# One head of wo on 64 partitions by eight small loads, w2's rows 8 to 13 in one slot, and LN2's sums on the vector engine, in a decode block on one core

## The chip, the core and the metric

The kernel runs on one NeuronCore of a Trainium2 chip. A core has TensorE (PE: matmuls; its weight loads are listed apart, as PEld), VectorE (DVE), ScalarE (ACT), GpSimd (POOL) and SyncE (SP, which here only issues DMAs), and sixteen DMA engines that move data from HBM to the on-chip memory (SBUF, 128 partitions). Matmuls write to PSUM. The metric is the device time of one execution in microseconds (us), the median of several runs.

## The reference, cut to what matters

Two sequences, one token each: a block with adaptive layer norm, attention over the last 4096 positions of a K/V cache, and a feed-forward with SiLU. All is fp32.

```python
def reference(A_x, A_k_cache, A_v_cache, A_wq, A_wo, B_x, B_w1, B_w2, c, w_mod):
    # B=2, D=512, 32 query heads, 8 KV heads, Dh=128, F=1792, window W=4096
    x = A_x
    mod = (silu(c) @ w_mod).reshape(2, 6, 1, -1)
    sa, ca, ga, sb, cb, gb = (mod[:, i] for i in range(6))
    h = layernorm(x) * (1 + ca) + sa
    x = x + ga * attention(h, A_k_cache, A_v_cache, A_wq, A_wo)   # last W keys; ends in  o @ wo
    h = layernorm(x) * (1 + cb) + sb                              # LN2
    return x + gb * (silu(h @ B_w1) @ B_w2)
```

The weights and the part of the caches that is read are 97.5 MB, each byte used once.

## The kernel before

Nearly all of the work is the loading. Every large load goes through one queue, SP's, into a ring of eight slots of 16 KB per partition (`slots`; `stream(n)` gives the next n). A load can be issued only when what stood in its slots has been read, so SP waits for PE before most loads. The order of the loads is w_mod, x, wq, then four groups (`grp` 0 to 3; a group is four KV heads of one sequence), for each group K and then V, 8 MB each in four slots, then wo in two loads (heads 0 to 23 and 24 to 31), w1 in two, and w2 in five: rows 0 to 7 of the fourteen that each partition holds, rows 8 to 10, 11, 12 and 13. `inorder` keeps an instruction in the order of the code on its engine.

For each group PE forms the scores (L281), softmax runs on DVE and ACT, PE forms the weighted sum of V (L326), and `collect` scales the result on ACT and turns it by PE into columns (`oT`, L345), which a copy puts into `oTn`: for each head a block of 128 partitions x 32 columns. After the last group:

- `acc_o` (L413): for each head q one matmul with `oTn[:, q]` stationary and the head's 512 columns of wo moving. The output goes to 32 of the 128 rows of `acc_o`, quarter g = q % 4, so that the four quarters of the array (32 columns each) can run side by side. The profile calls this shape 128*32.
- `gather` adds the four quarters up: ACT copies acc_o in two halves to `acc_o_sb` (L396), PE forms `ao` (L400). DVE turns it and forms `x1T`, the residual, as 128 x 4 x 2.
- LN2: `column_means` (L443) multiplies `x1T` with a matrix of 1/512 in four accumulating matmuls; `dT`, `hT` and `sq` follow on DVE. The product with w1 (`hid`, L459) runs on the unscaled h; the variance's `column_means` stands between its two halves, and the scale `rstd` comes in after the product.
- SiLU on DVE and ACT gives `uT` (L163).
- w2: the first WIDE = 11 rows go through `acc_yw` (L489), in quarters as with wo; ACT copies the sum to `y_sb` (L511). The last three rows are "turned" (L501): the weights are stationary and the two columns of uT move, sixteen small instructions for a row (eight for the first). The same is done with y_sb, between these rows. A scan on DVE (L522) and a store end it.
- `busy(n, ...)` puts n matmuls without use (L266, `junk`) on PE where it would wait. They write to rows 0 to 31, the first quarter.

Each fp32 matmul is two passes on PE and counts twice in the profile.

Of the kernel before, what the change touches and what calls it, by code (L numbers as in the profile page):

```python
# [8 lines left out]
F32 = mybir.dt.float32  # L9
# [4 lines left out]
P = 128  # L14
# [14 lines left out]
def adaln_block(  # L29
# [54 lines left out]

    def load_runs(w, per, lo, hi):

        e = w.shape[1]
        n = -(-(hi - lo) * e // 4096)
        t = stream(n)[:, : (hi - lo) * e].rearrange("p (q e) -> p q e", e=e)
        inorder(nc.sync.dma_start(t, w.rearrange("(p q) e -> p q e", q=per)[:, lo:hi, :]))  # L90
        return t
# [168 lines left out]

    oT = bank("O", "oT")[:, :64]
    STEPS = 4
# [72 lines left out]
    def collect(grp, o_ps, rl):  # L335

        o_sb = once.tile([P, 4 * DH], F32, tag="wide", name=f"ob{grp}")
        for c in (slice(0, D // 2), slice(D // 2, D)):
            nc.scalar.activation(o_sb[:, c], o_ps[:, c], AF.Copy, scale=rl)  # L339
        last = grp == STEPS - 1  # L340
        if last:
            busy(1, junk[0])
        cols = oT[:, 16 * grp : 16 * grp + 16]
        for v in range(4):
            inorder(nc.tensor.matmul(  # L345
                cols[:, 4 * v : 4 * v + 4],
                o_sb[:, v * DH : (v + 1) * DH],
                id4[:, 4 * v : 4 * v + 4],
                start=True,
                stop=True,  # L350
            ))
        b, n = divmod(grp, 2)
        (nc.vector.tensor_copy if last else nc.scalar.copy)(
            oTn[:, 16 * n : 16 * n + 16, 16 * b], cols
        )
# [3 lines left out]
    def load_wo(lo, hi):  # L359
        wt = load_runs(wo, 32, lo, hi)  # L360
        wot.extend(wt[:, q, :] for q in range(hi - lo))

    for grp in range(STEPS):
        s_ps = scores(grp)
        if grp < STEPS - 1:
            kt[grp + 1] = load_group(k_cache, grp + 1)
        else:
            load_wo(0, 24)
            load_wo(24, 32)
# [40 lines left out]
    busy(4, junk[0])  # L410
    for q in range(32):
        g = q % 4
        inorder(nc.tensor.matmul(  # L413
            acc[32 * g : 32 * g + 32, :],
            oTn[:, q, :],
            wot[q],
            start=(q < 4),
            stop=(q >= 28),
        ))
    gather(ao, acc, "acc_o_sb", True, True, fill=1)  # L420
    busy(1, junk[1])
    T2, WIDE = F // P, 11
    w2t = {}
    for lo, hi in ((0, 8), (8, 11), (11, 12), (12, 13), (13, T2)):
        wt = load_runs(w2, T2, lo, hi)
        for tt in range(lo, hi):
            w2t[tt] = wt[:, tt - lo, :]
    aoT = once.tile([P, 4, 32], F32, tag="zp", name="aoT")
# [10 lines left out]
    def column_means(t, name):  # L439

        m = bank("B", name)[:, :B]
        for k in range(4):
            inorder(nc.tensor.matmul(m, mean512, t[:, k, :], start=(k == 0), stop=(k == 3)))  # L443
        return m

    mean = column_means(x1T, "mean_b")
    busy(1, junk[1])
# [5 lines left out]
    sq = once.tile([P, 4, B], F32, tag="sq", name="sq")  # L453
    nc.vector.tensor_mul(sq, dT, dT)
    FC = F // 4
    hp = bank("A", "hid")[:, :FC]
    for k in range(4):
        for g in range(4):
            inorder(nc.tensor.matmul(  # L459
                hp[32 * g : 32 * g + 32, :],  # L460
                hT[:, k, :],
                w1t[k][:, g * FC : (g + 1) * FC],
                start=(k == 0),
                stop=(k == 3),
            ))
        if k == 1:
            var = column_means(sq, "var_b")
# [122 lines left out]
```

## Time and profile before

| what | value |
|---|---|
| time, median of 3 runs | 233.28 us (233.25 to 233.31) |
| the profiled execution | 233.04 us, its span 231.4 us |
| mean granted TensorE clock | 0.801 over the span, 1.00 from 202 us on |
| PE busy | 126.8 us (55%) |
| ACT, DVE, POOL busy | 19.7, 15.0, 7.7 us |
| DMA | 97.65 MB, mean 422 GB/s |

Span is the time from the first to the last instruction on the core. A row of a timeline has its start and its duration in us, the engine, the line of the code, the operation, out<-in and how many instructions were merged; behind it in brackets stands the idle time of the engine ahead of it and what ended that. "issue" means that the profile shows nothing that the engine waited for. Matmul durations overlap: a pass of 0.59 us leaves its part of the array earlier than that.

### The profile page before, as it was taken

How to read it: one execution, taken by the hardware profiler on the slowest of the kernel's cores; microseconds unless marked ns; L12 is line 12 of the kernel's file. 1: busy time of each engine (PE TensorE's matmuls, PEld its weight loads, DVE VectorE, ACT ScalarE, POOL GpSimd, SP SyncE). 2: the span in 40 equal slices, each digit the busy share in tenths (PEclk: the TensorE clock that was granted, in tenths of full speed). 3: DMA queues.
4: the chain of work that ended last, by engine and by line, in shares of the span. 5: the costliest groups of instructions: out<-in, count | busy, mean ns of one | idle time of the engine just before them, and what ended most of it. 6: DMA issues, size and time to landing. Idle time of an engine off the chain costs nothing.

```text
span 231.4 us, 2188 instructions
## 1 busy us (share of the span) xinstructions
PE 126.8 (55%) x982; PEld 45.9 (20%) x982; DVE 15.0 (6%) x44; ACT 19.7 (9%) x45; POOL 7.7 (3%) x28
## 2 busy tenths in 40 slices
PE   0005906831950781491096078139509607999986
PEld 0003301310210221121033012112202202345333
DVE  0004020000011000002000000100000200000130
ACT  0203010110040010001001000100100100000331
POOL 8102000000000000000000000000000000000000
PEclk9999995985796596598579659656957965999999
DMA  9998988989889898898999989999899999999993
GB/s 399 417 454 362 544 362 385 513 374 532 362 374 532 374 513 374 385 513 385 487 396 396 510 385 467 408 408 498 385 430 445 419 456 408 416 405 442 413 411 137
DMA packets 2915, 97.65 MB, mean 422 GB/s; under 512 B 460, under 2 KB 476, under 8 KB 1116
## 3 DMA queue, kind: packets, MB, share of 16 engines
q1 hardware_dynamic: 2748, 97.52, 97.9%
q8 instruction: 7, 0.11, 0.2%
q10 hardware_dynamic: 160, 0.01, 0.0%
HBM read 97.53 MB, written 0.01 MB: 421 GB/s over the span
## 4 chain that ended last, share of the span: by engine, by line
DMA 73%; PE 23%; POOL 2%; issue 1%; SPq 0%; ACT 0%; DVE 0%; POOLq 0%
DMA slots<-in_A_v_cache_dram 50%; PE o L326 16%; DMA slots<-in_A_wq_dram 13%; DMA slots<-in_B_w_dram 10%; PE q L235 4%; PE acc_yw L489 1%; PE yx L501 1%; PE qT L245 0%; POOL qs L136 0%; POOL oTn L140 0%; SPq L152 0%; ACT q_sb L243 0%; POOL warm L114 0%; POOL avg L104 0%; POOL same L108 0%
## 5 line engine op out<-in xcount | busy, mean ns | idle before, releaser
L326 PE MATMUL o<-slots,probs 128*32 128x512 f32 x256 | 37.9, 755 | 29.1 <-DMA slots<-in_A_v_cache_dram 29.1
L281 PE MATMUL s<-slots,qs 128*32 128x512 f32 x256 | 35.5, 718 | 32.3 <-DMA slots<-in_A_k_cache_dram 32.3
L326 PEld LDWEIGHTS o<-slots,probs 128*32 128x32 f32 x256 | 11.5, 131 | 52.2 <-issue 52.2
L281 PEld LDWEIGHTS s<-slots,qs 128*32 128x32 f32 x256 | 9.4, 130 | 55.2 <-issue 39.0
L235 PE MATMUL q<-slots,hq_T 128*32 128x512 f32 x64 | 9.2, 724 | 7.3 <-DMA slots<-in_A_wq_dram 7.3
L293 DVE TENSOR_REDUCE mx<-s 128x1 f32<-128x512 f32 x4 | 2.8, 691 | 140.5 <-PE s L281 140.5
L173 PE MATMUL mean_a<-mv_a,avg 128*128 128x1 f32 x2 | 0.6, 347 | 18.4 <-DVE mv_a L170 18.4
L266 PE MATMUL junk<-warm,id 128*32 128x512 f32 x20 | 9.6, 595 | 0.0
L339 ACT ACTIVATE ob<-o,rl 128x256 f32<-128x256 f32 x8 | 3.4, 470 | 69.4 <-PE o L326 69.4
L413 PE MATMUL acc_o<-slots,oTn 128*32 128x512 f32 x64 | 7.2, 593 | 0.0
L295 ACT ACTIVATE mp<-part,mx 128x8 f32<-128x8 f32 x4 | 1.2, 300 | 70.0 <-DVE mx L293 70.0
L209 PE MATMUL m_sp<-slots,scT 128*32 128x512 f32 x32 | 5.9, 827 | 0.0
L345 PE MATMUL oT<-id,ob 128*128 128x4 f32 x32 | 4.2, 255 | 1.9 <-ACT ob L339 1.9
L235 PEld LDWEIGHTS q<-slots,hq_T 128*32 128x32 f32 x64 | 2.3, 130 | 13.3 <-issue 13.2
L345 PEld LDWEIGHTS oT<-id,ob 128*128 128x128 f32 x32 | 3.9, 191 | 5.5 <-ACT ob L339 5.5
L308 PE MATMUL lp<-rowsum,same 128*128 128x1 f32 x8 | 1.7, 286 | 5.1 <-ACT pr L303 5.1
L206 PE MATMUL m_a<-slots,scT 128*32 128x256 f32 x32 | 3.6, 543 | 1.1 <-POOL scT L163 1.1
L413 PEld LDWEIGHTS acc_o<-slots,oTn 128*32 128x32 f32 x64 | 3.6, 110 | 3.3 <-issue 3.1
L173 PEld LDWEIGHTS mean_a<-mv_a,avg 128*128 128x128 f32 x2 | 0.5, 310 | 18.4 <-issue 18.4
L297 PE MATMUL mg<-mp,same 128*128 128x8 f32 x8 | 1.6, 266 | 4.6 <-ACT mp L295 4.6
L459 PE MATMUL hid<-slots,hT_b 128*32 128x448 f32 x32 | 3.4, 544 | 0.0
L489 PE MATMUL acc_yw<-slots,uT 128*32 128x512 f32 x22 | 2.8, 599 | 0.9 <-DMA slots<-in_B_w_dram 0.9
(95 smaller groups left out, 59.9 us busy)
## 6 DMA issues: line engine op xcount, KB each, us to landing
slots<-in_w_mod_dram SPq DMA_DIRECT2D x1, 6144.0 KB, 17.1
slots<-in_A_wo_dram SPq DMA_DIRECT2D x1, 6144.0 KB, 25.6
slots<-in_B_w_dram SPq DMA_DIRECT2D x1, 2688.0 KB, 17.8
slots<-in_A_wo_dram SPq DMA_DIRECT2D x1, 2048.0 KB, 29.6
slots<-in_B_w_dram SPq DMA_DIRECT2D x1, 2048.0 KB, 23.1
slots<-in_B_w_dram SPq DMA_DIRECT2D x1, 896.0 KB, 19.6
slots<-in_B_w_dram SPq DMA_DIRECT2D x1, 768.0 KB
slots<-in_B_w_dram SPq DMA_DIRECT2D x3, 256.0 KB, 16.0
```

The costliest lines, as they stand in the source:

```text
L206: nc.tensor.matmul(m_a[r, :], scT[:, k, :], ab[:, g], start=(k == 0), stop=(k == 3))
L209: nc.tensor.matmul(m_sp[r, :], scT[:, k, :], cd[:, g], start=(k == 0), stop=(k == 3))
L235: inorder(nc.tensor.matmul(q_ps[32 * g : 32 * g + 32, :], hq_T[:, k, :], wqt[:, k, lo : lo + 4 * DH], start=(k == 0), stop=(k == 3),))
L266: inorder(nc.tensor.matmul(unread[0:32, :], id4, warm, start=True, stop=True,))
L281: inorder(nc.tensor.matmul(s_ps[32 * c : 32 * c + 32, :], stat(grp, v, s), kt[grp][:, lo : lo + 512], start=(s == 0 and v == 0), stop=(s = ...
L293: nc.vector.tensor_reduce(mx, s_ps, axis=AX.X, op=ALU.max)
L326: inorder(nc.tensor.matmul(o_ps[r : r + 32, :], probs[grp % 2][:, 32 * n + 16 * s : 32 * n + 16 * s + 32], vt[grp][:, lo : lo + 512], star ...
L339: nc.scalar.activation(o_sb[:, c], o_ps[:, c], AF.Copy, scale=rl)
L345: inorder(nc.tensor.matmul(cols[:, 4 * v : 4 * v + 4], o_sb[:, v * DH : (v + 1) * DH], id4[:, 4 * v : 4 * v + 4], start=True, stop=True,))
L413: inorder(nc.tensor.matmul(acc[32 * g : 32 * g + 32, :], oTn[:, q, :], wot[q], start=(q < 4), stop=(q >= 28),))
L459: inorder(nc.tensor.matmul(hp[32 * g : 32 * g + 32, :], hT[:, k, :], w1t[k][:, g * FC : (g + 1) * FC], start=(k == 0), stop=(k == 3),))
L489: inorder(nc.tensor.matmul(yw[32 * g : 32 * g + 32, :], uT[:, tt, :], w2t[tt], start=(tt < 4), stop=(tt >= WIDE - 4),))
```

## The change

**One head of wo.** Head 27 (`SPLIT`) leaves the large wo tensor, which keeps 31 heads; its loads are now heads 0 to 23 of these 31 and the other seven. Head 27's 128 x 512 weights become a tensor `wo2` of eight pieces of 8 rows x 1024 elements (32 KB each), and after each of the eight K and V loads SP issues one of them, into eight partitions (p, p+4, ... p+28) of a new buffer `woh` of 64 partitions x 2 x 512. On SP, from the last group's loads to the last of w2, before:

```order
L82 DMA slots<-in_A_k_cache_dram 128x16384
L82 DMA slots<-in_A_v_cache_dram 128x16384
L90 DMA slots<-in_A_wo_dram 128x12288
L90 DMA slots<-in_A_wo_dram 128x4096
L90 DMA slots<-in_B_w_dram 128x5376
L90 DMA slots<-in_B_w_dram 128x1792
L90 DMA slots<-in_B_w_dram 128x4096
L90 DMA slots<-in_B_w_dram 128x1536
L90 DMA slots<-in_B_w_dram 128x512 x3
```

and now (5376 and 1792 are w1, what follows is w2):

```order
L84 DMA slots<-in_A_k_cache_dram 128x16384
L87 DMA woh<-in_A_wo_dram 8x1024
L84 DMA slots<-in_A_v_cache_dram 128x16384
L87 DMA woh<-in_A_wo_dram 8x1024
L98 DMA slots<-in_A_wo_dram 128x12288
L98 DMA slots<-in_A_wo_dram 128x3584
L98 DMA slots<-in_B_w_dram 128x5376
L98 DMA slots<-in_B_w_dram 128x1792
L98 DMA slots<-in_B_w_dram 128x4096
L98 DMA slots<-in_B_w_dram 128x1024
L98 DMA slots<-in_B_w_dram 128x512 x4
```

A small load now follows each K and each V load (those of the three earlier groups too), wo's second load is shorter by a head, and w2's rows 8 and 9 come as one load, the others alone. The large loads keep their order.

The head's output is needed on partitions 0 to 63 twice: its first 64 rows come there as they are, its last 64 rows by a fifth `oT` matmul in the groups 1 and 3, whose stationary window is shifted by 64 columns, as a 33rd block of `oTn`. In `acc_o` two matmuls over 64 partitions take the place of head 27's, at places 24 and 25, so that acc_o has 33 rows and its last one is in quarter 32 % 4 = 0.

On PE, from the turning of the last group's result to the gathering, before:

```order
L345 MATMUL oT<-id,ob_592 128x4 x4
L266 MATMUL junk_591<-warm,id 32x512 x4
L413 MATMUL acc_o<-slots,oTn 32x512 x32
L266 MATMUL junk_607<-warm,id 32x512
L400 MATMUL ao<-acc_o_sb,id 32x128 x4
L266 MATMUL junk_607<-warm,id 32x512
L443 MATMUL mean_b<-x1T,mean_87 128x2 x4
L266 MATMUL junk_607<-warm,id 32x512
L459 MATMUL hid<-slots,hT_b 32x448 x8
L443 MATMUL var_b<-sq,mean_87 128x2 x4
L459 MATMUL hid<-slots,hT_b 32x448 x8
L266 MATMUL junk_607<-warm,id 32x512 x2
```

and now:

```order
L365 MATMUL oT<-id,ob_602 128x1
L275 MATMUL junk_601<-warm,id 32x512 x4
L435 MATMUL acc_o<-slots,oTn 32x512 x24
L435 MATMUL acc_o<-woh,oTn 32x512 x2
L435 MATMUL acc_o<-slots,oTn 32x512 x7
L275 MATMUL junk_618<-warm,id 32x512
L419 MATMUL ao<-acc_o_sb,id 32x128 x4
L275 MATMUL junk_618<-warm,id 32x512
L470 MATMUL mean_b<-ks_mean_b,mean_87 128x2
L275 MATMUL junk_618<-warm,id 32x512
L487 MATMUL hid<-slots,hT_b 32x448 x8
L470 MATMUL var_b<-ks_var_b,mean_87 128x2
```

The two half rows stand inside acc_o, one oT matmul is added ahead of it, and mean_b and var_b have one matmul instead of four (the rows that end the piece are hid's second half and three junk matmuls instead of two).

**LN2's sums.** `column_means` first adds the four parts on DVE (`tensor_reduce`, 128x2 from 128x8) and then needs one matmul; for the variance the sum stands ahead of hid's first half in the code, the matmul where it was.

**w2.** Rows 8 to 13 go into one slot instead of four, in loads of rows 8 and 9, 10, 11, 12 and 13. WIDE is 10, so that row 10 is turned too. On PE at the end, before:

```order
L489 MATMUL acc_yw<-slots,uT 32x512 x11
L501 MATMUL yx<-uT,slots 64x2 x8
L501 MATMUL yx<-id,y_sb 32x2 x8
L501 MATMUL yx<-uT,slots 32x2 x16
L501 MATMUL yx<-id,y_sb 32x2 x8
L501 MATMUL yx<-uT,slots 32x2 x16
```

and now:

```order
L517 MATMUL acc_yw<-slots,uT 32x512 x10
L529 MATMUL yx<-uT,slots 64x2 x8
L529 MATMUL yx<-id,y_sb 32x2 x8
L529 MATMUL yx<-uT,slots 32x2 x16
L529 MATMUL yx<-id,y_sb 32x2 x8
L529 MATMUL yx<-uT,slots 32x2 x32
```

One row leaves acc_yw, and sixteen small matmuls are added behind the last part of y_sb.

The diff, without the host's rearranging of wo:

```diff
+SPLIT = 27
 def load_group(cache, grp):
     t = stream(4)
-    nc.sync.dma_start(t, cache[grp])
+    inorder(nc.sync.dma_start(t, cache[grp]))
+    i = 2 * grp + (cache is v_cache)
+    p = 32 * (i // 4) + i % 4
+    inorder(nc.sync.dma_start(
+        woh[p : p + 29 : 4, :, :].rearrange("p s e -> p (s e)"), wo2[i]
+    ))
     return t
...
-    oTn = const([P, 32, 32], "oTn")
+    woh = const([P // 2, 2, D], "woh")
+    oTn = const([P, 33, 32], "oTn")
...
     # collect
-    cols = oT[:, 16 * grp : 16 * grp + 16]
+    b, n = divmod(grp, 2)
+    per = 16 + n
+    cols = oT[:, 17 * grp : 17 * grp + per]
...
+    if n:
+        v = SPLIT % 16 // 4
+        inorder(nc.tensor.matmul(
+            cols[:, 16:17],
+            o_sb[:, v * DH + DH // 2 : v * DH + DH // 2 + DH],
+            id4[:, SPLIT % 16 : SPLIT % 16 + 1],
+            start=True, stop=True,
+        ))
...
-    for q in range(32):
-        g = q % 4
+    heads = [q for q in range(HQ) if q != SPLIT]
+    parts = [(oTn[:, q, :], wot[i]) for i, q in enumerate(heads)]
+    parts[24:24] = [(oTn[: P // 2, q, :], woh[:, i, :]) for i, q in enumerate((SPLIT, HQ))]
+    for i, (o, w) in enumerate(parts):
+        g = i % 4
         inorder(nc.tensor.matmul(acc[32 * g : 32 * g + 32, :], ...))
...
-    T2, WIDE = F // P, 11
-    for lo, hi in ((0, 8), (8, 11), (11, 12), (12, 13), (13, T2)):
-        wt = load_runs(w2, T2, lo, hi)
+    T2, WIDE = F // P, 10
+    wt = load_runs(w2, T2, 0, 8)
+    ends = stream()[:, : (T2 - 8) * D].rearrange("p (q e) -> p q e", e=D)
+    for lo, hi in ((8, 10), (10, 11), (11, 12), (12, 13), (13, T2)):
+        load_runs(w2, T2, lo, hi, ends[:, lo - 8 : hi - 8, :])
...
     def column_means(t, name):
+        ks = once.tile([P, B], F32, tag=f"ks_{name}", name=f"ks_{name}")
+        nc.vector.tensor_reduce(ks, t.rearrange("p k b -> p b k"), axis=AX.X, op=ALU.add)
         m = bank("B", name)[:, :B]
-        for k in range(4):
-            inorder(nc.tensor.matmul(m, mean512, t[:, k, :], start=(k == 0), stop=(k == 3)))
-        return m
+        return m, lambda: inorder(nc.tensor.matmul(m, mean512, ks, start=True, stop=True))
...
-    busy(2, junk[1])
+    busy(3, junk[1])
     hidT = ...
```

More of the change, by code (lines that the diff above doesn't have):

```diff
@@ L36, in adaln_block @@
     wo: bass.AP,
+    wo2: bass.AP,
     w1: bass.AP,
@@ L81, in load_group, with load_runs @@
         t = stream(4)
-        nc.sync.dma_start(t, cache[grp])
+        inorder(nc.sync.dma_start(t, cache[grp]))
[4 more added lines that the diff above has]
+        ))
         return t
-    def load_runs(w, per, lo, hi):
+    def load_runs(w, per, lo, hi, t=None):
         e = w.shape[1]
-        n = -(-(hi - lo) * e // 4096)
-        t = stream(n)[:, : (hi - lo) * e].rearrange("p (q e) -> p q e", e=e)
+        if t is None:
+            n = -(-(hi - lo) * e // 4096)
+            t = stream(n)[:, : (hi - lo) * e].rearrange("p (q e) -> p q e", e=e)
         inorder(nc.sync.dma_start(t, w.rearrange("(p q) e -> p q e", q=per)[:, lo:hi, :]))
@@ L259, in adaln_block @@
     stat = lambda grp, v, s: qs[:, 256 * grp + 64 * v + 32 * s : 256 * grp + 64 * v + 32 * s + 32]
-    oT = bank("O", "oT")[:, :64]
+    oT = bank("O", "oT")[:, :68]
     STEPS = 4
@@ L351, in collect @@
             ))
-        b, n = divmod(grp, 2)
+        if n:
[4 more added lines that the diff above has]
+                id4[:, SPLIT % 16 : SPLIT % 16 + 1],
+                start=True,
+                stop=True,
+            ))
         (nc.vector.tensor_copy if last else nc.scalar.copy)(
-            oTn[:, 16 * n : 16 * n + 16, 16 * b], cols
+            oTn[:, 16 * n : 16 * n + per, 16 * b], cols
         )
@@ L359, in load_wo @@
     def load_wo(lo, hi):
-        wt = load_runs(wo, 32, lo, hi)
+        wt = load_runs(wo, HQ - 1, lo, hi)
         wot.extend(wt[:, q, :] for q in range(hi - lo))
@@ L368, in adaln_block @@
             load_wo(0, 24)
-            load_wo(24, 32)
+            load_wo(24, HQ - 1)
         rl = softmax(grp, s_ps)
@@ L410, in adaln_block @@
     busy(4, junk[0])
-    for q in range(32):
-        g = q % 4
+    heads = [q for q in range(HQ) if q != SPLIT]
[3 more added lines that the diff above has]
+        g = i % 4
         inorder(nc.tensor.matmul(
             acc[32 * g : 32 * g + 32, :],
[L415 to L418, printed above, removed]
+            o,
+            w,
+            start=(i < 4),
+            stop=(i >= len(parts) - 4),
         ))
@@ L421, in adaln_block @@
     busy(1, junk[1])
-    T2, WIDE = F // P, 11
+    T2, WIDE = F // P, 10
     w2t = {}
-    for lo, hi in ((0, 8), (8, 11), (11, 12), (12, 13), (13, T2)):
-        wt = load_runs(w2, T2, lo, hi)
+    wt = load_runs(w2, T2, 0, 8)
+    for tt in range(8):
+        w2t[tt] = wt[:, tt, :]
+    ends = stream()[:, : (T2 - 8) * D].rearrange("p (q e) -> p q e", e=D)
+    for lo, hi in ((8, 10), (10, 11), (11, 12), (12, 13), (13, T2)):
+        load_runs(w2, T2, lo, hi, ends[:, lo - 8 : hi - 8, :])
         for tt in range(lo, hi):
-            w2t[tt] = wt[:, tt - lo, :]
+            w2t[tt] = ends[:, tt - 8, :]
     aoT = once.tile([P, 4, 32], F32, tag="zp", name="aoT")
@@ L439, in column_means @@
     def column_means(t, name):
+        ks = once.tile([P, B], F32, tag=f"ks_{name}", name=f"ks_{name}")
+        nc.vector.tensor_reduce(ks, t.rearrange("p k b -> p b k"), axis=AX.X, op=ALU.add)
         m = bank("B", name)[:, :B]
-        for k in range(4):
-            inorder(nc.tensor.matmul(m, mean512, t[:, k, :], start=(k == 0), stop=(k == 3)))
-        return m
-    mean = column_means(x1T, "mean_b")
+        return m, lambda: inorder(nc.tensor.matmul(m, mean512, ks, start=True, stop=True))
+    mean, product = column_means(x1T, "mean_b")
+    product()
     busy(1, junk[1])
@@ L454, in adaln_block @@
     nc.vector.tensor_mul(sq, dT, dT)
+    var, product = column_means(sq, "var_b")
     FC = F // 4
@@ L466, in adaln_block @@
         if k == 1:
-            var = column_means(sq, "var_b")
+            product()
             std = once.tile([P, B], F32, tag="stdb", name="std_b")
@@ L525, in adaln_block @@
     tc.no_tile_sem_insts.add(store.ins.name)
-_INS = ["A_x", "A_k_cache", "A_v_cache", "A_wq", "A_wo", "B_w1", "B_w2", "c", "w_mod"]
+_INS = ["A_x", "A_k_cache", "A_v_cache", "A_wq", "A_wo", "A_wo2", "B_w1", "B_w2", "c", "w_mod"]
 def kernel(**inputs):
@@ L536 @@
     from concourse.bass_utils import run_bass_kernel_spmd as _run
-    inputs = {name: _np.asarray(inputs[name]) for name in _INS}
+    inputs = {name: _np.asarray(inputs[name]) for name in _INS if name in inputs}
     for name, order in (("A_k_cache", "keys"), ("A_v_cache", "values")):
@@ L550 @@
     inputs["B_w2"] = inputs["B_w2"].reshape(F, P, 4).transpose(0, 2, 1).reshape(F, D)
-    inputs["A_wo"] = inputs["A_wo"].reshape(HQ, DH, D).transpose(1, 0, 2).reshape(HQ * DH, D)
+    a = inputs["A_wo"].reshape(HQ, DH, D)
+    inputs["A_wo"] = _np.delete(a, SPLIT, axis=0).transpose(1, 0, 2).reshape((HQ - 1) * DH, D)
+    a = a[SPLIT].reshape(2, 2, 8, 4, D).transpose(1, 3, 2, 0, 4)
+    inputs["A_wo2"] = a.reshape(8, 8, 2 * D)
     arrays = {f"in_{name}_dram": _np.ascontiguousarray(inputs[name]) for name in _INS}
```

## The prediction

> **What bounds the kernel now.** I read the profile's table of DMA queues first, then the chain that ended last in order of time, then the DMA activity of the last 2.4 us, and last the timeline from 195 us on, row by row.
>
> The queue table and the last rows of the chain:
>
> ```profile
> q1 hardware_dynamic: 2748, 97.52, 97.9%
> q8 instruction: 7, 0.11, 0.2%
> ...
> 164.07 28.40 DMA slots<-in_A_v_cache_dram
> ...
> 202.15 23.05 DMA slots<-in_B_w_dram
> 225.20 0.14 issue
> 225.34 2.82 PE acc_yw L489 x22
> 228.16 1.56 PE yx L501 x91
> 229.72 0.02 issue
> 229.74 0.19 DVE yo L522
> ```
>
> One queue keeps the sixteen DMA engines busy for 97.9% of the span, so what stands ahead of the last bytes can only gain by moving bytes between the engines; what can gain besides is the stretch behind the load of w2's rows 0 to 7, which lands at 202.15 + 23.05 = 225.20. From there PE runs to 229.7.
>
> The DMA activity from 226.6 to 229.0 us, 40 slices of 0.06 us, tenths of sixteen engines:
>
> ```profile
> DMA  9997996945333443344334334332332110000000
> ```
>
> Up to 227.1 all sixteen work; from 227.2 to 228.5 only three to four tenths of them do: five or six engines end 1.3 us behind the rest, and a load has landed only with its last engine. The seven instruction packets of 16 KB in the queue table are of that number and size; that they made the late engines late is likely, not shown by these rows.
>
> The timeline from the products with wo to the end (start, duration, engine, line; x counts passes, two for each fp32 instruction):
>
> ```profile
> 202.81 0.97 PEld L345 LDWEIGHTS oT<-id,ob 128*128 128x128 f32 x8 [0.84 <-ACT ob L339]
> 203.79 3.62 PE L266 MATMUL junk<-warm,id 128*32 128x512 f32 x8
> 204.25 0.11 PEld L266 LDWEIGHTS junk<-warm,id 128*32 128x32 f32 x1 [0.32 <-issue]
> 204.68 0.11 PEld L266 LDWEIGHTS junk<-warm,id 128*32 128x32 f32 x1 [0.32 <-issue]
> ...
> 207.09 7.19 PE L413 MATMUL acc_o<-slots,oTn 128*32 128x512 f32 x64
> 214.42 0.65 ACT L396 COPY acc_o_sb<-acc_o 128x256 f32<-128x256 f32 x2 [11.38 <-PE acc_o L413]
> 216.14 0.17 DVE L432 TENSOR_TENSOR x1T<-x1T,xcT 128x8 f32<-128x8 f32 x1
> 216.36 0.97 PEld L443 LDWEIGHTS mean_b<-x1T,mean 128*128 128x128 f32 x8 [1.05 <-DVE x1T L432]
> 217.34 1.05 PE L266 MATMUL junk<-warm,id 128*32 128x512 f32 x2
> 217.45 0.16 DVE L449 TENSOR_TENSOR dT<-x1T,mean_b 128x8 f32<-128x8 f32 x1 [1.15 <-PE mean_b L443]
> 217.65 0.17 DVE L450 SCALAR_TENSOR_TENSOR hT_b<-modT,dT 128x8 f32<-128x8 f32 x1
> 218.36 1.71 PE L459 MATMUL hid<-slots,hT_b 128*32 128x448 f32 x16
> 220.00 0.97 PEld L443 LDWEIGHTS var_b<-sq,mean 128*128 128x128 f32 x8 [0.73 <-issue]
> 220.99 1.71 PE L459 MATMUL hid<-slots,hT_b 128*32 128x448 f32 x16
> 222.51 1.88 PE L266 MATMUL junk<-warm,id 128*32 128x512 f32 x4
> 224.93 0.20 DVE L163 TENSOR_TENSOR uT<-z,sgh 128x28 f32<-128x28 f32 x1
> 227.10 0.15 PEld L489 LDWEIGHTS acc_yw<-slots,uT 128*32 128x32 f32 x6 [0.75 <-DMA slots<-in_B_w_dram]
> 228.27 0.65 ACT L511 COPY y_sb<-acc_yw 128x256 f32<-128x256 f32 x2 [3.95 <-PE acc_yw L489]
> 228.70 0.31 PE L501 MATMUL yx<-id,y_sb 128*32 128x2 f32 x16
> 229.25 0.42 PE L501 MATMUL yx<-uT,slots 128*32 128x2 f32 x30
> ```
>
> The junk rows give the price of a pass in one quarter of the array (32 columns): 204.68 - 204.25 = 0.43 us. acc_o has 64 of them in 7.19 us, so the four quarters run side by side, sixteen passes each (6.9 us). uT ends at 225.13, the load of w2 at 225.20: two chains, PE's from wo on and the queue's, meet within 0.1 us. The third thing is the stall at 227.10, where PE waits for rows 8 to 10.
>
> **The change part by part**, along PE's chain first, in the times of this execution.
>
> *The fifth oT product* of the last group: two passes of a 128-wide load, which follow each other in (0.97 - 0.19)/7 = 0.11 us (the last of the eight takes 0.19). The four busy instructions behind it start 0.22 later. They fill the first quarter alone, before until 203.79 + 8 x 0.43 = 207.23; now until 207.45. The wo load lands at 206.95, so it's this quarter's free time that counts: +0.22. In the second group the same product lies in the wait for the next K load.
>
> *The 33rd row of wo.* Rows go to quarter i % 4, so the last one is the first quarter's ninth: two passes that nothing runs beside, +0.86, not the 0.22 that 1/32 of 7.19 would suggest.
>
> *The two half rows* work on 64 partitions, in another shape of the array than the rows around them. No row of this trace has that shape. The nearest are changes of its width: the eighth load of mean_b starts at 216.36 + 7 x 0.11 = 217.14, and junk only at 217.34, 0.09 more than the usual step. Lower bound nothing, since the quarters may stay independent (a gain is excluded: a pass of 512 columns is no shorter for fewer rows); upper bound 0.2 for each of two changes. I take 0.1 each, by those rows: +0.2.
>
> [...]
>
> So acc_o_sb starts 1.28 later, 215.70.
>
> *The mean.* Six passes of 0.11 go, -0.67. A reduction on DVE comes ahead of PE:
>
> ```profile
> L301 DVE TENSOR_REDUCE bias<-mg x4: 166/167/167, 67.6 to 183.7; 128x1 f32<-128x8 f32 x4
> ```
>
> It has eight elements too: 0.17 and the 0.03 between two DVE instructions (216.14 + 0.17 to 216.34), +0.20. Net -0.47; dT starts at 217.45 + 1.28 - 0.47 = 218.26, and hT is ready 0.37 later, 218.63.
>
> *The first half of hid* started at 218.36, though hT was ready at 217.82: it waited for w1's load. Its landing and the others' come from these issues (last number: us to landing):
>
> ```profile
> 181.35 0.33 SPq L90 DMA_DIRECT2D slots<-in_A_wo_dram  x1
> 200.38 0.80 SPq L90 DMA_DIRECT2D slots<-in_B_w_dram  x2
> ...
> slots<-in_A_wo_dram SPq DMA_DIRECT2D x1, 6144.0 KB, 25.6
> slots<-in_B_w_dram SPq DMA_DIRECT2D x1, 2688.0 KB, 17.8
> ```
>
> 181.35 + 25.6 = 206.95 and 200.38 + 17.8 = 218.2. That wait hid 0.4 us of the chain; now hT is what is late. And the busy instruction behind the mean holds the first quarter for 0.02 + 2 x 0.43 from 217.34 + 0.81 on, to 219.04. The variance's product needs all quarters, so 219.04 counts: +0.68.
>
> *The variance*: six passes less, -0.67; its reduction lies beside hid. The second half starts at 220.99 + 0.68 - 0.67 = 221.00, and everything on DVE and ACT behind it follows at +0.01: uT ends at 225.14. The third busy instruction takes 2 x 0.43 on PE, which waits for uT there anyway: four passes lay in that wait before and were through at 222.51 + 4 x 0.43 = 224.23, 0.9 ahead of uT. Without that cover it would cost 0.86.
>
> *acc_yw* then starts 0.08 behind uT (the steps from DVE to a load and to its product, 0.05 and 0.03), at 225.22, if w2 has landed: -0.12. It has ten rows, three in the first quarter, as before with eleven: the last pass starts 5 x 0.43 later and takes 0.59, end 227.96 against 228.16. Rows 8 and 9 now come in one load of 512 KB, 32 KB for each engine, 1.2 us at the 434 GB/s of the windows below, so at 226.4, before PE gets to them at 226.9: the stall at 227.10 is gone. -0.20.
>
> *The fourth turned row*: 32 passes. Thirty of them took 0.42 with a last one of 0.17, 0.0084 each: +0.27, on the path, since the copy y_sb gates the first of what is left and the rest follows without a gap.
>
> Sum: -0.20 + 0.27 = **+0.07 us**; with the half rows' bounds -0.13 to +0.27.
>
> *The queue.* The eight small loads cost SP 0.33 each, between waits of 10 to 30 us; nothing stands behind them but the next K or V load, which waits for PE in any case. Their waits are for loads at least three K or V loads back, and the half rows' product waits for all eight, the last of them behind v3: all landed by 207. Bytes move: one head is 256 KB, 16 KB for each of sixteen engines less in wo, 32 KB more for each of eight, or 16 KB more if all sixteen share the small loads. A full window gives the rate of an engine:
>
> ```profile
> 86.00:115.00 29.00, 10.23 (x78) 3.65 (x76) 1.62 (x4) 2.11 (x6) 0.00 (x0) 0.71 1.01 434
> 226.60:227.10 0.50, 0.50 (x8) 0.00 (x1) 0.00 (x0) 0.00 (x0) 0.00 (x0) 1.00 1.04 385
> ```
>
> 434/16 = 27 GB/s, 0.6 us for 16 KB; the second row, with 2 KB packets alone, has the engines just as full. So the w2 load lands 0.6 us earlier if the late engines are among the eight relieved, unchanged if all share, 0.6 later if one late engine carries small loads. No view groups packets by engine; followed one by one, the packets of c's small load went through engines other than nearly all of those that an instruction packet held up. I take 0.6 earlier. Before wo's last piece the early engines have 1.3 us in hand for at most 8 x 4 KB, 1.2 us, so K and V land as before. None of it comes off the time in the sum: uT is now last, at 225.14 against 224.60. Row 13 lands before 229 and is used from 229.2.
>
> The profiled execution took 233.04 us, 0.24 under the median 233.28; +0.07 on the median is 233.35, say 233.3.
>
> **The rivals.**
>
> *A late engine carries the small loads* (slower). The place is the landing of w2's rows 0 to 7: 225.80; acc_yw starts 0.14 behind, 0.60 later than before, ends 0.52 later (the stall is gone), and the turned row adds 0.27: +0.79, 234.1. It decides from a landing at 225.1 on. For it: five or six of sixteen are late, one is enough. Against it: what the single packets say. 0.10.
>
> *The small loads do nothing for the late engines*: landing 225.20, acc_yw at 225.34, end 228.08, +0.19, 233.5. 0.08, within the bound.
>
> *The queue was the limit all along and PE's chain is shorter than my sum*, as the chain's 23.05 us of DMA speaks for: acc_yw starts with the landing, 224.74, ends at 227.48, -0.68 + 0.27 = -0.41, 232.9. Against it: the ninth row in one quarter, which follows from the code. 0.17, half of it past the bound, if the late engines gain more than 0.6.
>
> *Small loads hold their engines for more than their bytes.* [...] The row of 2 KB packets speaks against it, though those follow each other in one load. 0.03. [...]
>
> **How the numbers follow.** My sum holds with 0.62. Faster or slower by over 0.2% is 0.47 us, about what a measurement of this kernel can tell from no change. Sum, unchanged landing and half the third rival are within it: 0.62 + 0.08 + 0.08 = 0.78, less some for what I didn't see on either side: 0.68. Faster 0.15; slower 0.17 (first and last rival, and the unseen). The range goes from the third rival to the first, 232.8 to 234.1.
>
> **What would show it.** [...] mean_b's gap from x1T to dT shrinks by 0.47. hid's second half starts within 0.2 of 221.0. acc_yw's wait is ended by uT, not by DMA: if DMA ends it near 225.3 or 225.9, the second or first rival holds. No stall inside acc_yw. DMA activity at the end falls from ten tenths to none within 0.6 us rather than 1.3. [...]

## The result, and the profile after

| | before | after |
|---|---|---|
| median | 233.22 us (233.01 to 233.31, 6 runs) | 235.70 us (235.05 to 236.02, 6 runs) |
| profiled execution, its span | 233.04, 231.4 us | 235.34, 233.8 us |
| store, issue to landing | 1.4 us | 2.8 us |

The change costs 2.4 us: the ratio is 1.0104, 95% interval 1.0089 to 1.0119. That lies outside the predicted range, on the slower side. Three runs of the kernel of a2_k16 and c3_k16_again below took 1.9 to 4.8% longer than its fastest, for a reason that is not known, and are left out of the figures.

The queue table of the changed kernel (queue, kind: packets, MB, share of the sixteen engines) has one packet of instructions more than before:

```profile
q1 hardware_dynamic: 3020, 97.52, 97.0%
q8 instruction: 8, 0.13, 0.2%
```

The end of the chain that ended last (start, duration):

```profile
173.87 7.53 PE s L290 x56
181.41 26.82 DMA slots<-in_A_wo_dram
208.37 8.18 PE acc_o L435 x66
...
223.63 2.56 PE junk L275 x6
226.18 2.71 PE acc_yw L517 x20
228.89 1.81 PE yx L529 x107
230.73 0.19 DVE yo L550
```

Before, the last DMA on this chain was w2's load, up to 225.20. Now it is wo's first load, which lands at 181.41 + 26.82 = 208.23 instead of 206.95, and everything behind it is work of PE and DVE. The rows of the timeline that answer to those of the prediction:

```profile
204.35 3.62 PE L275 MATMUL junk<-warm,id 128*32 128x512 f32 x8
...
208.37 5.36 PE L435 MATMUL acc_o<-slots,oTn 128*32 128x512 f32 x48 [0.40 <-DMA slots<-in_A_wo_dram]
...
213.66 0.14 PEld L435 LDWEIGHTS acc_o<-woh,oTn 64*32 64x32 f32 x4 [0.84 <-issue]
...
214.64 0.16 PEld L435 LDWEIGHTS acc_o<-slots,oTn 128*32 128x32 f32 x8 [0.84 <-issue]
...
216.39 1.02 PE L275 MATMUL junk<-warm,id 128*32 128x512 f32 x2
...
216.67 0.65 ACT L415 COPY acc_o_sb<-acc_o 128x256 f32<-128x256 f32 x2 [13.29 <-PE acc_o L435]
...
218.39 0.17 DVE L458 TENSOR_TENSOR x1T<-x1T,xcT 128x8 f32<-128x8 f32 x1
...
219.23 0.16 DVE L476 TENSOR_TENSOR dT<-x1T,mean_b 128x8 f32<-128x8 f32 x1 [0.48 <-PE mean_b L470]
...
219.43 0.17 DVE L477 SCALAR_TENSOR_TENSOR hT_b<-modT,dT 128x8 f32<-128x8 f32 x1
...
221.91 1.71 PE L487 MATMUL hid<-slots,hT_b 128*32 128x448 f32 x16
...
225.86 0.21 DVE L172 TENSOR_TENSOR uT<-z,sgh 128x28 f32<-128x28 f32 x1
...
226.12 2.77 PE L517 MATMUL acc_yw<-slots,uT 128*32 128x512 f32 x20
...
228.99 0.65 ACT L539 COPY y_sb<-acc_yw 128x256 f32<-128x256 f32 x2 [3.74 <-PE acc_yw L517]
...
230.73 0.19 DVE L550 TENSOR_TENSOR_SCAN yo<-g,yx 128x16 f32<-128x16 f32 x1 [4.66 <-PE yx L529]
```

The scan starts at 230.73 instead of 229.74, +0.99. The span grew by 2.4. The rest lies behind the scan, in the store. What the DMA engines moved from 226.6 us to the end in 40 slices, before (to 232, slices of 0.135 us) and after (to 234, slices of 0.185 us), with the packets of instructions after, and the issue of the store (last number: us to landing):

```profile
GB/s 410 410 334 304 167 152 137 167 152 137 167 137 106 121 46 0 0 0 0 0 0 0 0 0 0 0 0 0 0 0 0 43 18 0 0 0 0 0 0 0
...
out_dram<-yo ACTq DMA_DIRECT2D x1, 8.0 KB, 1.4
```

```profile
GB/s 288 299 399 310 299 244 133 66 44 55 44 55 33 22 0 0 0 0 0 0 0 0 0 0 0 0 0 89 40 2 0 0 2 1 0 44 0 0 0 0
...
q8 instruction: 2, 0.03, 1.9%
...
out_dram<-yo ACTq DMA_DIRECT2D x1, 8.0 KB, 2.8
```

Before, the last thing that moves is the store, (43 + 18) x 0.135 = 8 KB. After, (89 + 40 + 2) x 0.185 = 24 KB move there: the store's 8 KB and one more packet of 16 KB, the second of instructions in this stretch, at 231.6 to 232.0. In the trace's single packets it starts at 231.74 and takes 0.92; fifteen of the store's sixteen parts have landed by 232.4, the last one at 233.79. The store's own packets tell why: most are through at 232.01, the last nine follow only behind 232.66, where the packet of instructions ends. (The lone 44 behind, 8 KB, is a packet of q14; the other traces looked at have one near the end too, most of them behind the span.)

So there are two questions: what made wo's load and the chain behind it late (about 1.0 us at the scan), and whether it is the eighth packet that costs the rest.

### The profile page after: what moved, and what is told of

Same layout as the page of the kernel before. It is cut to its first block, busy times and chain, and to the rows that moved or that the text cites. A ratio compares the mean times of both kernels' runs of the same rounds, so it can differ in the third digit from the quotient of the medians.

```text
span 233.8 us, 2254 instructions
## 1 busy us (share of the span) xinstructions
PE 127.2 (54%) x1008; PEld 44.5 (19%) x1008; DVE 15.4 (7%) x46; ACT 19.7 (8%) x45; POOL 7.7 (3%) x28
## 4 chain that ended last, share of the span: by engine, by line
DMA 66%; PE 28%; POOL 3%; DVE 1%; issue 1%; ACT 0%; DVEq 0%; POOLq 0%
DMA slots<-in_A_k_cache_dram 50%; PE s L290 15%; DMA slots<-in_A_wo_dram 11%; DMA xc<-in_A_x_dram 5%; PE acc_o L435 3%; PE m_sp L218 2%; PE junk L275 2%; PE hid L487 1%; PE m_a L215 1%; PE acc_yw L517 1%; PE yx L529 1%; DVE sgc L171 0%; POOL qs L144 0%; POOL oTn L149 0%; POOL sgc L168 0%
## 5 line engine op out<-in xcount | busy, mean ns | idle before, releaser
L290 PE MATMUL s<-slots,qs 128*32 128x512 f32 x256 | 36.4, 733 | 32.8 <-DMA slots<-in_A_k_cache_dram 32.8
L335 PE MATMUL o<-slots,probs 128*32 128x512 f32 x256 | 36.5, 731 | 29.1 <-DMA slots<-in_A_v_cache_dram 29.1
L275 PE MATMUL junk<-warm,id 128*32 128x512 f32 x22 | 10.5, 595 | 0.0
L435 PEld LDWEIGHTS acc_o<-slots,oTn 128*32 128x32 f32 x62 | 2.2, 109 | 5.4 <-issue 4.2
```

The lines of the kernel that those rows point to most:

```text
L275: inorder(nc.tensor.matmul(unread[0:32, :], id4, warm, start=True, stop=True,))
L290: inorder(nc.tensor.matmul(s_ps[32 * c : 32 * c + 32, :], stat(grp, v, s), kt[grp][:, lo : lo + 512], start=(s == 0 and v == 0), stop=(s = ...
L335: inorder(nc.tensor.matmul(o_ps[r : r + 32, :], probs[grp % 2][:, 32 * n + 16 * s : 32 * n + 16 * s + 32], vt[grp][:, lo : lo + 512], star ...
L435: inorder(nc.tensor.matmul(acc[32 * g : 32 * g + 32, :], o, w, start=(i < 4), stop=(i >= len(parts) - 4),))
```

## The experiments

My theory after the result: (A) the small loads, which land in eight parts each where a large one lands in sixteen, go to some of the sixteen engines; where one of these is already late, wo lands later by all that it carried, and PE's longer row of work follows from there; (B) PE's program is now so long that the profile shows an eighth packet of instructions, at the end, and the store waits for it. The rivals: the fourth turned row costs more than the 0.27 of its passes; PE's 33 rows cost by themselves; LN2's sums or the one slot for w2 cost. Median and ratio are against the kernel before on the same chip (233.13 to 233.22 us).

### The fourth turned row and the eighth packet

**b1_idle15**, the kernel before with small matmuls where PE waits, far from the end:

```diff
+        if grp == 1:
+            idle = bank("B", "idle")
+            for _ in range(15):
+                inorder(nc.tensor.matmul(idle[0:32, :2], id4, warm[:, :2], start=True, stop=True))
```

> The kernel before with fifteen tiny matmuls (two columns, 60 passes and weight loads) put where PE waits for a K load after the second group; nothing else is changed. Theory (the eighth block of PE instructions is fetched when PE's program is some 50 records longer, and it is fetched right in front of the store): an eighth instruction packet in the DMA table, the store lands 2.8 us after its issue instead of 1.4, time 234.6 against 233.2. Rival (the late store of the changed kernel comes from its small loads, or was chance): seven packets or eight with no effect, store in 1.4 us, 233.2.

234.08 us, ratio 1.0042 (1.0029 to 1.0055). Its DMA queues and the issue of the store:

```profile
q8 instruction: 8, 0.13, 0.2%
...
out_dram<-yo ACTq DMA_DIRECT2D x1, 8.0 KB, 2.6
```

Matmuls that nothing waits for make the kernel 0.9 us slower, with an eighth packet and a store of 2.6 us. The cost was a little less than I expected.

**a1_wide11**, the changed kernel with three turned rows, as before:

```diff
-    T2, WIDE = F // P, 10
+    T2, WIDE = F // P, 11
-    for lo, hi in ((8, 10), (10, 11), (11, 12), (12, 13), (13, T2)):
+    for lo, hi in ((8, 11), (11, 12), (12, 13), (13, T2)):
```

> The changed kernel with WIDE = 11 and rows 8 to 10 in one load again: three turned rows, 60 PE records fewer; small loads, half rows, the one slot and LN2's sums stay. Theory: no eighth instruction packet, store in 1.4 us (-1.4); the fourth turned row's 0.27 comes off; wo's first load still lands near 208.2 and acc_yw still starts near 226.1. 235.7 - 1.7 = 234.0. Rival (the store is late from the small loads): 235.4.

234.06 us, 1.0041 (1.0029 to 1.0053). Two rows of its timeline, then its DMA queues and the store:

```profile
208.35 5.42 PE L435 MATMUL acc_o<-slots,oTn 128*32 128x512 f32 x48
...
226.16 2.77 PE L517 MATMUL acc_yw<-slots,uT 128*32 128x512 f32 x22
```

```profile
q8 instruction: 7, 0.11, 0.2%
...
out_dram<-yo ACTq DMA_DIRECT2D x1, 8.0 KB, 1.4
```

The late wo stays (it lands at 208.21; acc_o starts at 208.35, about when PE's busy matmuls end too), the eighth packet and 1.6 us are gone. But this edit takes the row away too, so it doesn't tell B from its rival.

**c4_busy3less**, the changed kernel with three busy matmuls fewer, to shorten PE's program:

```diff
-    gather(ao, acc, "acc_o_sb", True, True, fill=1)
+    gather(ao, acc, "acc_o_sb", True, True)
-    busy(1, junk[1])          # behind the mean
-    busy(3, junk[1])
+    busy(2, junk[1])
```

> The changed kernel with three busy instructions fewer (the one in the gathering, the one behind the mean, one of the three behind hid): 12 PE records fewer, four turned rows and the small loads stay. Theory: the first quarter isn't held for 0.86 behind the mean, hid starts with hT, -0.35; the eighth instruction packet, which came with PE's last few records, is not fetched, -1.3: 234.05. If 12 records are too few, the packet stays and the time is 235.3. Rival (the store is late for another reason): 235.3 with seven packets.

235.47 us, 1.0093 (1.0080 to 1.0106): nothing gained. Its DMA queues from 226.6 us on, past the span's end:

```profile
q8 instruction: 2, 0.03, 1.6%
...
out_dram<-yo ACTq DMA_DIRECT2D x1, 8.0 KB, 1.4
```

There are still two packets in this stretch. In the trace the eighth starts at 234.36, behind the store, outside the span of 232.1 us; yet the execution took 235.34, 3.2 us more than its span, against 1.5 in the changed kernel and 1.9 in a1_wide11. So the eighth packet seems to cost about as much behind the store as in front of it; what the end of the execution waits for there no view shows. The profiled run of the changed kernel is then the exception: four of its other five runs took 2.4 to 2.8 us beyond spans of 233.2 and 233.3, where no run of a kernel with seven packets took more than 2.0. Those runs have no trace; that the packet came behind the store in them is likely, not shown.

**f1_fewer_opening** keeps all four turned rows and shortens the program at the start. It leaves out half of the opening's products of the modulation, so its output is not the block's; PE waits for the load of wq behind them either way:

```diff
-    for k in range(4):        # m_a, m_sp
+    for k in (0, 3):
```

> The changed kernel with all four turned rows and eight small loads, but with the opening's products of the modulation (m_a and m_sp) for k = 0 and 3 only; those for k = 1 and 2, 16 matmuls of 64 instructions of TensorE in the trace, are left out. They lie at the start, ahead of the first wq products, where TensorE waits for loads, so nothing on the path of the end changes but the length of TensorE's program, about 1973 instructions instead of 2037 (1977 in the run of three turned rows, 1983 before). Theory (the length of the program calls for an eighth packet of 16 KB of instructions, and that packet costs most of what the fourth turned row seems to cost): seven such packets, the store 1.4 us to landing, 234.1 to 234.6 us, that is the run of three turned rows and 0.1 to 0.3 for the row itself. Rival (the fourth turned row, or the split of w2's loads that comes with it, costs 1.5 by itself): eight or seven packets, 235.4 to 235.9 us.

234.38 us, 1.0058 (1.0044 to 1.0071).

Its DMA queues and store, then its timeline:

```profile
q8 instruction: 7, 0.11, 0.2%
...
out_dram<-yo ACTq DMA_DIRECT2D x1, 8.0 KB, 1.7
```

```profile
225.58 2.77 PE L517 MATMUL acc_yw<-slots,uT 128*32 128x512 f32 x20 [0.27 <-DMA slots<-in_B_w_dram]
```

With the fourth row and without the eighth packet the loss falls from 2.4 to 1.2 us; the two ratios' intervals lie apart. B holds: the packet costs 1.0104 - 1.0058, 1.1 us, and the row with its split load 1.0058 - 1.0041, 0.4 (priced at 0.27; the intervals overlap). Its profiled run (233.71) was the fastest of the five; in it acc_yw waits for w2 and wo landed by 207.1, so at wo no engine was both late and loaded. The other four took 234.35 to 234.72. So f1 may also have gained by which engines were late. The profiled runs of c4 and f1 answer that: wo landed at 207.0 and 207.1, the spans are 232.1 and 232.2, and yet c4, with the eighth packet, took 1.6 us longer. With 0.9 in b1, the packet's price is known only roughly.

The trace has 1983 records of PE (matmuls, weight loads and some twenty others) before, 1977 in a1, 1973 in f1: seven packets. It has 2025 in c4, 2037 after, 2042 in b1: eight. No run lies between. Each packet has 16 KB. In b1 the only one behind 226.6 comes at about 230.4, in front of the store (78 GB/s in one slice of 0.21 us there, 16 KB), and b1 took 0.9 us more than the kernel before.

### What is left: 0.9 us

**a3_bigwo**, a1 without the small loads: all of wo in the large loads, 32 whole rows; LN2's sums, the one slot and the third busy instruction stay.

```diff
-    parts[24:24] = [(oTn[: P // 2, q, :], woh[:, i, :]) for i, q in enumerate((SPLIT, HQ))]
+    parts = [(oTn[:, q, :], wot[q]) for q in range(HQ)]
-        wt = load_runs(wo, HQ - 1, lo, hi)
+        wt = load_runs(wo, HQ, lo, hi)
```

> As the kernel with WIDE = 11, but without the small loads: head 27 is back in the large loads and in one matmul, 32 rows of acc_o, four oT matmuls. LN2's sums on DVE, the one slot for w2's rows 8 to 13 and the third busy matmul stay. Theory: wo's first load lands at 207.0, acc_o ends as before, PE's chain to uT is 0.7 shorter than before (0.67 in var; the 0.47 of the mean goes into the wait for w1), acc_yw waits for w2's load at 225.2, and rows 8 to 10 again at 227.1: time as before, 233.2. Rival (LN2's sums or the one slot cost time): 233.6 or more.

233.34 us, 1.0008 (0.9999 to 1.0016). Three rows of its timeline:

```profile
207.17 7.07 PE L417 MATMUL acc_o<-slots,oTn 128*32 128x512 f32 x64 [0.15 <-DMA slots<-in_A_wo_dram]
...
214.35 0.65 ACT L399 COPY acc_o_sb<-acc_o 128x256 f32<-128x256 f32 x2 [11.71 <-PE acc_o L417]
...
225.41 2.80 PE L499 MATMUL acc_yw<-slots,uT 128*32 128x512 f32 x22 [0.82 <-DMA slots<-in_B_w_dram]
```

PE now waits 0.82 us for w2: LN2's sums made its chain shorter, and nothing came of it, since the load is last. They neither cost nor gain anything that could be measured.

**d1_halves**, a3 with head 27 multiplied as two half rows out of the large load, 33 rows:

```diff
+    heads = [q for q in range(HQ) if q != SPLIT]
+    parts = [(oTn[:, q, :], wot[q]) for q in heads]
+    parts[24:24] = [(oTn[h : h + H, SPLIT, :], wot[SPLIT][h : h + H]) for h in (0, H)]   # H = 64
```

> The kernel with all of wo in the large loads (a3_bigwo, 233.34 us), but TensorE multiplies head 27 as two half rows of 64 partitions, so 33 rows and two changes of tile form, as in the changed kernel; no small load. Theory (the change loses its time because late loads and TensorE's longer row of work follow each other): without the late loads the copy of acc_o ends 1.1 to 1.2 later (215.5 against 214.35), the work from there to uT takes what it took in the run of three turned rows (216.71 to 225.90, 9.2), so uT is there at 224.7, and acc_yw still starts at 225.4, when w2's load lands: 233.2 to 233.5 us. Rival (TensorE's extra row costs by itself, whatever the loads do): 0.8 to 1.2 more than a3_bigwo, 234.1 to 234.5.

233.46 us, 1.0014 (1.0005 to 1.0023). Its timeline:

```profile
216.18 0.65 ACT L399 COPY acc_o_sb<-acc_o 128x256 f32<-128x256 f32 x2 [12.46 <-PE acc_o L422]
...
225.36 0.21 DVE L165 TENSOR_TENSOR uT<-z,sgh 128x28 f32<-128x28 f32 x1
225.64 2.81 PE L504 MATMUL acc_yw<-slots,uT 128*32 128x512 f32 x22
```

acc_o_sb comes 1.8 later than in a3 (216.18 against 214.35; I expected 1.2, the rest is a later start of acc_o), and acc_yw only 0.2: the slack ahead of w2 takes up the rest. PE's longer work without the small loads costs 0.1 to 0.2 us; with them, in a1, 0.0041 - 0.0014 more, 0.6. So PE's part alone is not the loss: the late wo uses up the slack, and what follows adds. The small loads alone, with 32 whole rows, were not run; in a1 w2's rows 0 to 7 land at 225.77 against 225.27 in a3, which would cost about 0.5 by itself, an estimate from these two landings. No view groups landings by engine. In the trace fourteen of the sixteen parts of wo's first load land at 205.27 to 206.94 in the changed kernel, two at 207.84 and 208.24, as two at 208.03 and 208.21 in a1; before, five late ones end at 206.47 to 206.95. Two parts carry both delays: that is A's picture. The trace also confirms what made engines late, which the prediction called likely. In the loads before, one more of the sixteen parts lands over 1 us behind the rest from each instruction packet on: one behind the packet at 40.8 us, two behind 81.5, three behind 103.7, four behind 142.4, five behind 178.5. Each of these packets takes 0.92 to 0.97 us and has a 64 KB packet of 2.89 to 2.92 us beside it, where most take 2.42.

### Can the head be loaded otherwise?

**a2_k16** and **c3_k16_again** are one kernel: a1 with four small loads of 16 rows, so that all sixteen engines share them.

```diff
+        if cache is k_cache:
+            inorder(nc.sync.dma_start(
+                woh[grp : grp + 61 : 4, :, :].rearrange("p s e -> p (s e)"), wo2[grp]
+            ))
```

> As the kernel with WIDE = 11, but the small loads are four of 16 rows (64 KB), after the K loads alone, so that their rows can go over sixteen engines instead of eight: 16 KB more for each engine ahead of wo and 16 KB less in wo. Theory (wo's first load is late because engines held up by an instruction packet also carry 32 KB of small loads): wo's first load lands 0.6 later than in the kernel before, 207.6 instead of 208.2, w2's first load near 225.2 instead of 225.8, time 0.6 below the kernel with WIDE = 11, 233.4. Rival (a small load costs its engines more than its bytes, whatever it is spread over): four loads of 64 KB leave the landing at 208 or later, 234.0.

> The kernel with four small loads of 16 rows once more, for a profile without the disturbance that the first one fell into. Theory: v3 near 193.1, wo's first load at 207.6, the time near the 234.4 of its other runs would then have to come from PE's chain; if instead wo lands at 208 or later, its small loads cost more than their bytes.

They took 234.1 to 234.5 us, 1.0051 (1.0038 to 1.0064): no better than a1, where I had expected 233.4. The timeline of the second one has acc_o as late as a1's (the row is cut off at 212 us):

```profile
208.49 4.06 PE L434 MATMUL acc_o<-slots,oTn 128*32 128x512 f32 x35
```

**c1_one64** and **c2_one64_early**: a1 with one load of 64 rows of 4 KB instead of eight, between wo's two loads, or behind the first V load.

```diff
             load_wo(0, 24)
+            inorder(nc.sync.dma_start(woh.rearrange("p s e -> p (s e)"), wo2))   # c1
             load_wo(24, HQ - 1)
...
+        if grp == 0 and cache is v_cache:                                        # c2
+            inorder(nc.sync.dma_start(woh.rearrange("p s e -> p (s e)"), wo2))
```

> As the kernel with WIDE = 11, but head 27 comes in a single load of 64 rows x 4 KB between wo's two loads: no small loads ahead of K, V and wo, 16 KB for each of sixteen engines, PE's 33 rows and LN2's sums as in the change. Theory (PE's part of the prediction's sum was right, the landings were wrong): v3 and wo land as before (207.0), acc_yw starts near 225.3, 233.2 + 0.07 - 0.27 = 233.0 to 233.3. Rival (the half rows or the ninth row in one quarter cost more than priced): acc_yw near 226, 234.0.

> The same single load, issued right behind the first V load: 16 KB more for each of sixteen engines ahead of all that follows, 16 KB less in wo. Theory (bytes are what counts): v3 and wo's first load land 0.6 later than before (193.1 and 207.6), PE's chain 0.4 later than with the load between wo's two, w2's first load at 225.2 as before: 233.4 to 233.6. Rival (a load between the K and V loads costs more than its bytes, as the kernel with four loads of 16 rows suggests, 234.5): 234 or more.

235.37 us, 1.0091 (1.0076 to 1.0107), and 235.44 us, 1.0101 (1.0082 to 1.0120): both missed, by 2 us. Rows of the timelines, first of c1, then of c2 (its fastest run, 234.46):

```profile
208.44 5.36 PE L431 MATMUL acc_o<-slots,oTn 128*32 128x512 f32 x48 [1.42 <-DMA slots<-in_A_wo_dram]
...
227.47 1.92 PE L513 MATMUL acc_yw<-slots,uT 128*32 128x512 f32 x16 [0.75 <-DMA slots<-in_B_w_dram]
```

```profile
208.82 5.36 PE L432 MATMUL acc_o<-slots,oTn 128*32 128x512 f32 x48 [0.36 <-DMA slots<-in_A_wo_dram]
...
226.57 2.77 PE L514 MATMUL acc_yw<-slots,uT 128*32 128x512 f32 x22
```

16 KB for each engine should take 0.6 us, by the 2.42 that 64 KB take. These loads cost more than their bytes, and the packets of the trace say where: in a1 each packet of 4 KB takes 0.16 us, in c2 the median is 0.23 and the longest 0.47. My next theory was that the rows lie in one half of the partitions. Three kernels on one chip, all with products in 32 whole rows as in a3:

**d2_full128**: head 27 by one load of 128 rows of 2 KB over all partitions, behind the first V load.

```diff
+        if grp == 0 and cache is v_cache:
+            inorder(nc.sync.dma_start(woh, wo2))        # woh: 128 x 512
+    parts[24:24] = [(oTn[:, SPLIT, :], woh)]
```

> The kernel with all of wo in the large loads, but head 27 by one load of its own, 128 rows of 2 KB over all partitions, right behind the first V load; products in 32 whole rows. Theory (a load costs its bytes unless its rows lie on half of the partitions): everything between it and wo is 0.6 later (16 KB an engine at the 2.42 us that 64 KB take), wo's first part lands 0.6 later than in a3_bigwo and acc_o starts at 207.7; w2's loads come when they came, acc_yw at 225.4: 233.3 to 233.5 us. Rival (any load of another form between the large ones costs 1 to 1.5 on all engines, as the one of 64 rows did): acc_o at 208.5, acc_yw at 226.3: 234.2 to 234.8.

**e1_extra_low** and **e2_extra_every2**: a3 with one more load, which nothing reads; the two differ only in the partitions that its 64 rows go to.

```diff
+            inorder(nc.sync.dma_start(spare[0 : P // 2, :], wo2))     # e1
+            inorder(nc.sync.dma_start(spare[0 : P : 2, :], wo2))      # e2
```

> a3_bigwo with one load more, which nothing reads: 64 rows of 4 KB into partitions 0 to 63, right behind the first V load. It is the control of the next kernel. By its bytes everything behind it, w2's loads too, is 0.6 later: acc_yw at 226.0 and 233.9 to 234.0 us. By what the single load of 64 rows did (c2_one64_early), 1.5 later: acc_yw at 226.9 and 234.7 to 234.9 us.

> The same extra load of 64 rows of 4 KB, into every second partition from 0 to 126, so that its rows are spread over all partitions. Theory (rows that all lie on half of the partitions slow each other): 0.6 later by bytes, 233.9 to 234.0 us, and its packets take 0.16 us each. Rival (a load of 64 rows of 4 KB is slow wherever it goes, or any extra load is): as e1_extra_low, 234.7 to 234.9 us.

d2 took 233.32 us, 1.0007 (0.9998 to 1.0016), as a3 did: a load of its own for the head costs nothing that could be measured. e1 took 235.20 us, 1.0089 (1.0075 to 1.0102), 0.3 above the most I had expected, e2 234.06 us, 1.0040 (1.0027 to 1.0052), about as expected. Timelines of d2, e1 and e2, in this order:

```profile
225.57 2.79 PE L505 MATMUL acc_yw<-slots,uT 128*32 128x512 f32 x22 [0.81 <-DMA slots<-in_B_w_dram]
```

```profile
208.90 7.08 PE L421 MATMUL acc_o<-slots,oTn 128*32 128x512 f32 x64 [0.73 <-DMA slots<-in_A_wo_dram]
...
227.20 2.81 PE L503 MATMUL acc_yw<-slots,uT 128*32 128x512 f32 x22 [0.75 <-DMA slots<-in_B_w_dram]
```

```profile
207.95 7.37 PE L421 MATMUL acc_o<-slots,oTn 128*32 128x512 f32 x64
...
226.13 2.80 PE L503 MATMUL acc_yw<-slots,uT 128*32 128x512 f32 x22 [0.77 <-DMA slots<-in_B_w_dram]
```

Against a3's 225.41, acc_yw starts 0.7 later in e2, about the price by bytes (0.6), and 1.8 later in e1. The same rows from the same place cost 1.1 us more when they all go to partitions 0 to 63. In e2 every packet of 4 KB took 0.16 us, in e1 up to 0.34. For each engine the extra load's packets took 0.24 us more in e1 than in e2, and the 64 KB packets 0.77 more, those beside the extra load up to 3.69, where in e2 they took at most 2.44. Why the rows in the lower half slow each other and their neighbours stays open. In c3, whose rows of four partitions' distance also lie in 0 to 63, the 64 KB packets beside the small loads took 2.60 to 2.68 instead of 2.42, 0.7 in sum for an engine. In a1, whose loads of eight rows lie on 32 partitions each, the 64 KB packets took no more in sum than in the kernel before. So the half of the partitions can't be the whole condition, and no run varied it for loads of 8 or 16 rows.

No version here beats the kernel before by what can be measured; a3 and d2 stand at 233.3.

## Why the prediction was wrong

**The step that failed first** is the queue's: "Before wo's last piece the early engines have 1.3 us in hand for at most 8 x 4 KB, 1.2 us, so K and V land as before." It allowed small loads to the early engines only. By the landings of wo's parts (207.84 and 208.24, the other fourteen by 206.94) two engines were both late and loaded, and wo landed 1.28 us later, as much as the eight small packets take (8 x 0.16 = 1.27). The last V load landed at 193.59 instead of 192.47. "I take 0.6 earlier" for w2 fell with it: 225.81, 0.6 later. I had seen a single earlier load's engines miss those of the instruction packets and read a rule from it. The engines that an instruction packet holds up seem not to be the same in every profiled run: those of c4 and f1, with the same small loads, had wo by 207.1.

**The first rival** named the mechanism, "a late engine carries the small loads", and w2's load landed where it said, at 225.81 against its 225.80. But it put the whole price there, where the bytes taken off wo pay half of it back. At wo none has been paid back, and acc_yw's wait was ended by uT (226.07), not by DMA. So the rival was right in mechanism and too small: 0.79 against 0.99 at the scan, or 0.52 without the turned row against a1's 0.87. The 0.10 for it was too low: with five of sixteen engines late and eight loaded, no overlap would need a rule that keeps them apart.

**Not in the sum at all** was the length of PE's program. The queue table with its seven packets stood in the prediction, as what makes engines late. That the added passes, 64 of them for the turned row alone when its weight loads are counted, could call for an eighth was not asked. It cost 1.1 us, more than any one term of the sum.

**PE's own steps** held. The fifth oT product: the busy matmuls start 1.21 behind the first oT load instead of 0.98, +0.23 (0.22 in the sum), though acc_o waited for wo's load now, not for them. acc_o's first quarter runs from 208.37 to 216.39, 8.02 us: 18 passes of 0.43 are 7.74, so the ninth row is there, and 0.28 are left for the two changes of shape (0.2 taken, bounds 0 and 0.4). The rows show them one by one: the pass ahead of the half rows starts at 208.37 + 11 x 0.43 = 213.10 and would hand over at 213.53, the half rows load at 213.66; their two passes end at 214.52, the next load is at 214.64. That is 0.13 and 0.12. The half rows' single passes took 0.59 to 0.61 us, as those over 128 partitions do (0.59 to 0.62), so the added time lies at the two changes. From x1T to dT it is 0.84 instead of 1.31, -0.47 as priced. From hT's end, 219.60, to hid's second half 2.31 (2.37 in the sum). From y_sb to the scan 1.74 instead of 1.47, +0.27 as priced. No stall inside acc_yw. The scan's +0.99 is the sum's +0.07 and the 0.92 by which acc_o started later than the sum had it (208.37 against 207.45).

The small loads' issues on SP took 0.65 us each, not 0.33, and nothing waited for them, as the prediction had it.

**Small loads that hold their engines for more than their bytes** (0.03) did not happen with loads of eight rows: 0.16 us a packet. It did happen with loads of other shapes (c2, e1, c3 above).

In ratios to before, as far as the runs share them out: LN2's sums and the slot 0.0008, the 33 rows 0.0006, the small loads 0.0027 (with the fifth oT product), the fourth turned row 0.0017, the eighth packet 0.0046; together 0.0104. Each step is a difference of two ratios, in part from different chips, and the first two are no larger than their intervals. The time beyond the span is in these shares too, and it differs between kernels with seven packets, 1.6 us before, 1.9 in a1 and a3, 1.5 in f1, for a reason that no view shows.

## What to carry to other kernels

Look at the instruction packets in the queue table before adding matmuls: in b1 fifty-nine more records of PE, far ahead of the end, brought an eighth packet and cost 0.9 us. A load that uses only some of the DMA engines is to be priced as if it fell on the latest engine, and at the first load behind it that PE waits for, not at the last: here that was wo, 1.28 us late. The head's 256 KB were better spread over all partitions: d2's 128 rows of 2 KB cost nothing that could be measured, where the kernels with 64 rows of 4 KB in the lower half (c1, c2, e1) were 2 us slower.

## What the runs showed of the hardware that I had not expected

- With an eighth packet of 16 KB of instructions in front of it the store took 2.8 us (the changed kernel) and 2.6 (b1), instead of 1.4 to 1.7; in the changed kernel the last of its sixteen parts landed behind that packet, at 233.79, the others by 232.4. In c4, where it came behind the store, the execution went 3.2 us beyond its span, against 1.5 to 1.9.
- In the kernel before, each instruction packet ahead of wo made one more of a load's sixteen parts land over 1 us late, and it stayed late: five at wo, 206.47 to 206.95, against 205.45 at the latest for the rest. Which engines these are seems to differ between profiled runs: with the same small loads wo's first load ended at 207.0 and 207.1 (c4, f1) or at 208.2 (the changed kernel, a1).
- The same 64 rows of 4 KB cost 1.1 us more on partitions 0 to 63 than on every second of all 128, most of it in the 64 KB packets beside them (up to 3.69 us instead of 2.42).
- The change from products over 128 partitions to products over 64 took PE 0.13 us in the changed kernel, the change back 0.12.
